# Shifted copies by 64-bit adds on GpSimd, with GpSimd's other work moved to VectorE, in a two-layer attention and MLP kernel

## The chip, the core and the metric

The kernel runs on one core of a Trainium2 chip. The metric is the device time of one execution in microseconds (us). The profile calls the engines PE (TensorE), ACT (ScalarE), DVE (VectorE), POOL (GpSimd) and SP (SyncE); PEld is TensorE's weight load.

## What is computed

The input `x` is 2048 rows of 512 bf16 numbers. Two layers follow, each an attention block and an MLP block with a residual sum around each; both layers use the same weights.

```python
x = x + _A_ref(_layernorm(x), A_wqkv, A_wo)
x = x + _B_ref(_layernorm(x), B_w1, B_b1, B_w2, B_b2)
x = x + _A_ref(_layernorm(x), A_wqkv, A_wo)
x = x + _B_ref(_layernorm(x), B_w1, B_b1, B_w2, B_b2)
...
scores = jnp.einsum("bhqd,bhkd->bhqk", q, k) * (Dh ** -0.5)
p = _softmax(scores, axis=-1)
o = jnp.einsum("bhqk,bhkd->bhqd", p, v)
...
h = _gelu(jnp.einsum("bsd,df->bsf", x, w1) + b1)
```

There are 32 heads of 16 columns, and the MLP is 1792 wide. Softmax is over 2048 keys for each of 2048 queries, 32 heads and 2 layers: 268 million exponentials.

## The kernel before

**Score blocks.** Queries are taken in segments of 512 (the last of the second layer in two of 256). A pass covers a segment and eight heads' worth of columns in pairs; its unit is a cell, a 128x512 block of scores: 128 keys against 512 columns of query. A matrix product of 32 rows (`score`, L1324) writes each cell to a PSUM bank; the kernel has 4096 of them. The queries it multiplies are masked copies of Q, so that one half of the head pair is zero (`qpad`, L1272).

**Two ways to an exponential.** Most cells are exponentiated by ACT (`exps`, L1725), two or three cells to an instruction. The cells of five key tiles per layer (`KD`) may take another path, called D here. DVE reads the cell from PSUM and makes a uint16 number by one multiply and add (`dfirst`, L1480): the bits of a bf16 number near the exponential. `dchain` then makes three more copies, the first plus 32, 64 and 96 in the bits: one operation adds `SHIFT` (32) to copy 0 for copy 1 (POOL, L1565), one adds 64 to copies 0 and 1 for copies 2 and 3 (DVE, L1570). A buffer (`DU`) holds the four copies of two cells, or of one. PE multiplies each of the four copies with V scaled by a weight of its own (`VC`, made by `vcopies`, L1255, on POOL; products at L1791) and sums them, so that the errors of the four approximations cancel in part. An ACT cell needs one such product, a D cell four. Where a round of four products has fewer than four, products with zeros fill it (L1799); L1312 are filling products that keep PE busy.

**The rest.** `ln` makes layer norms: statistics on DVE (L719, L721), variance plus epsilon (L724), its power -0.5 on POOL (L726), the shift (L729), and the normalized rows (`ln_tile`, L747) on POOL, or on DVE for the first four tiles and the last two (`quick`). The rows go through a DMA transpose that SP issues (L751). `norm` divides the attention output by its sums: transpose (L910), reciprocal (L913), product (L920, most of them on POOL), transpose back (L929). `proj`, `wo`, `hpair` and `ytile` are the dense products (L598), read out of PSUM by DVE; GELU is ACT's (L1076). `init` sets constants, among them the ones column of V (L623, L628), on POOL.

**What sets the order.** Nothing is decided on the chip: `_Sched` plays all work as threads at build time, each operation with a cost in us, a priority and the keys that it reads and writes, and picks for each engine what starts first. What comes out is a fixed program for each engine, with semaphore waits. The planner knows that a `port` operation of DVE and an operation of POOL hold each other up (`_ready`). `PICKS` names, for each 24 us of ACT's clock, one of the eleven rows of settings in `ORDERS`, so it chooses among orders. Which cells go to D is decided there too: `attach`, `solo` and `next_d` give a cell to D where a bank and a buffer are free and DVE is not too far behind. SP issues every DMA, 405 entries in its program with the branches.

Of the kernel before, what the change touches and what calls it, by code (L numbers as in the profile page):

```python
# [5 lines left out]
ALU = mybir.AluOpType  # L6
ACT = mybir.ActivationFunctionType
BF16 = mybir.dt.bfloat16
F32 = mybir.dt.float32
F16 = mybir.dt.float16  # L10
U16 = mybir.dt.uint16

# [6 lines left out]
NL = 2  # L19
# [15 lines left out]
LNP = 7  # L35
# [48 lines left out]
PSHIFT = 3  # L84
# [15 lines left out]
PICKS = (2, 0, 0, 6, 8, 2, 5, 1, 0, 5, 1, 0, 7, 5, 1, 0, 0, 7, 2, 5, 9, 1, 8, 7,  # L100
         4, 5, 7, 7, 7, 8, 5, 0, 5, 6, 9, 9, 7, 0, 5, 2, 5, 3, 3, 7, 4, 2, 7, 2,
         0, 9, 7, 7, 3, 3, 0, 2, 10, 10, 4, 4)
# [3 lines left out]
SHIFT = 32  # L106
VW = (0.83984375, 0.70703125, 0.59375)
# [106 lines left out]
class _Op:  # L214
    __slots__ = ("eng", "cost", "fns", "reads", "writes", "sem", "by", "tail", "prio", "mode", "slack", "late", "back", "port", "limit", "after")

    def __init__(self, eng, cost, fns, reads=(), writes=(), sem=None, by=1, tail=0.0, prio=None, mode="F", slack=None):
# [6 lines left out]
        self.port = eng == "dve" and self.writes[:1] != [] and self.writes[0].startswith(("OTT", "NMR"))  # L224
# [20 lines left out]
class _Sched:  # L245
# [152 lines left out]
    def run(self):  # L398
        while True:
# [67 lines left out]
            if e == "pool":  # L467
                self.pool_ops.append((start, start + cost))
# [7 lines left out]
def bass_interleave_layers__mha_block__dense_activation_gelu__prompt_kernel(  # L476
# [13 lines left out]
    NT = S // 128  # L490

    with ExitStack() as es:
# [48 lines left out]
        T["NHALF"] = sb([128, 4], F32, "nhalf")  # L541
        T["STATS"] = sb([128, NT, 6], F32, "stats")
# [45 lines left out]
class _Plan:  # L588
# [12 lines left out]
    def init(self):  # L601
# [14 lines left out]
        yield _Op("pool", 0.3, lambda e: e.memset(T["B2row"][:], 0.0), writes=["B2zero"])  # L616
        yield _Op("dve", 0.6, lambda e: e.memset(self.bank(PVB), 0.0), writes=["B.%d" % PVB])
# [3 lines left out]
        yield ("need", ("lnt", 3, 0))  # L621
        for a in range(0, self.NT, 4):
            yield _Op("pool", 0.65, lambda e, a=a: e.memset(T["V"][0][:, a:a + 4, :, 16:17], 1.0), writes=["V01"])  # L623
        yield ("need", ("otn", 0, (0, 0, 512), 3))
        for a in range(0, self.NT, 4):
            if a == 8:
                yield ("need", "v1back")
            yield _Op("pool", 0.65, lambda e, a=a: e.memset(T["V"][1][:, a:a + 4, :, 16:17], 1.0),  # L628
                      writes=[self.vone(1, a)] + (self.dukeys(DV1) if a >= 8 else ["PART.0.%d" % g for g in range(8)]))
        yield ("give", "v1ones")  # L630

# [80 lines left out]
    def ln(self, tiles, dst, dkeys, prio, quick=False, gate=None):  # L712
# [4 lines left out]
        for t in tiles:  # L717
# [8 lines left out]
        yield _Op("pool", 0.37 + 0.18 * n, lambda e: e.tensor_tensor(  # L726
            out=T["RSTD"][:, sl], in0=T["VARR"][:, sl], in1=T["NHALF"][:, 0:n], op=ALU.pow),
            reads=["VARR.%d" % c, "NHALF"], writes=["RSTD.%d" % c])
# [8 lines left out]
    def ln_tile(self, c, t, dst, dkeys, quick):  # L737
# [8 lines left out]
        eng, cost = ("dve", 0.4) if quick else ("pool", 0.77)  # L746
        yield _Op(eng, cost, lambda e: e.tensor_scalar(  # L747
# [130 lines left out]
    def norm(self, l, seg, g, b, part, final):  # L878
# [37 lines left out]
        pool = g < 6 and seg[2] == 512  # L916
        nb = w // 32
        for i, t in enumerate(ts):
            o3 = T["OTT"][:, o, 0:w].rearrange("p (k c) -> p k c", c=32)[:, :, 16 * t:16 * t + 16]
            yield _Op(*(("pool", 0.63 * w / 512) if pool else ("dve", 0.153 + 0.262 * w / 512)), lambda e, i=i, o3=o3: e.tensor_tensor(  # L920
# [297 lines left out]
    def setup_attention(self):  # L1218
# [25 lines left out]
        self.rush = self.base[(NL - 1, self.segs[-1][-3])]  # L1244
        self.duleft, self.open, self.starved, self.lend = {}, None, 0, 2

    def vcopies(self):
        T = self.T
        for l in range(NL):
            yield ("cond", lambda l=l: self.pv >= self.lead[l])  # L1250
            for j, kt in enumerate(KD[l]):
                yield ("need", ("V", l, kt, kt // 4))
                src = T["V"][l][:, kt, :, :].rearrange("p h c -> p (h c)")
                for i, w in enumerate(VW):
                    yield _Op("pool", 0.68, lambda e, j=j, i=i, w=w, src=src: e.tensor_scalar(  # L1255
# [5 lines left out]
    def qpad(self):  # L1261
        T = self.T
        for pi, (l, seg, g, kts, part, final) in enumerate(self.pas):
# [7 lines left out]
            for i, t in enumerate(ts):  # L1271
                yield _Op("pool", 0.27 + 0.42 * w / 512, lambda e, s=s, q=q, i=i, t=t, w=w: e.tensor_scalar(  # L1272
# [278 lines left out]
    def dchain(self, pair):  # L1551
# [3 lines left out]
        cells, du = pair["cells"], pair["du"]  # L1555
        yield ("cond", lambda: len(cells) == self.cap[du] or pair["full"] or self.starved)
# [6 lines left out]
        if self.s.clock["pool"] <= self.s.clock["dve"] + PSHIFT and len(pair["cells"]) == n:  # L1563
            a, b = U[:, 0, 0:n, :].rearrange("p j q -> p (j q)"), U[:, 1, 0:n, :].rearrange("p j q -> p (j q)")
            one = _Op("pool", 0.15 + 0.45 * n, lambda e, a=a, b=b: e.tensor_scalar(b, a, float(SHIFT), 1.0, op0=ALU.add, op1=ALU.mult),  # L1565
                      reads=key[0], writes=key[1])
        else:
# [333 lines left out]
```

## Time and profile before

| | |
|---|---|
| time, median of 3 runs | 1490.49 us (1490.07 to 1491.15) |
| span of the profiled execution | 1488.6 us |
| ACT busy | 1458.5 us (98%) |
| PE busy | 1439.3 us (97%) |
| DVE busy | 1369.4 us (92%) |
| POOL busy | 857.7 us (58%) |

The span runs from the first instruction to the last of one profiled execution; the 1.9 us between it and the median lie outside of it. A row of a group view gives line, engine, operation, what it writes and reads, the shapes and the count; then busy time in us and the mean of one in ns; then the idle time of its engine just before, and who ended it. A row of a line view gives the shortest, median and longest duration in ns. A row of a wait view reads: who waited, for whom, us in total, times, the longest.

### The profile page before, as it was taken

To read this page: it belongs to the slowest core of one execution; us is meant where nothing else is said; L and a number is where in the kernel's file an instruction comes from. 1 tells how busy PE (TensorE), PEld (TensorE's weight loads), DVE (VectorE), ACT (ScalarE), POOL (GpSimd) and SP (SyncE) were. 2 spreads that over 40 slices of the span, in tenths; PEclk is the share of its full clock that TensorE was granted. 3 is DMA by queue.
4 is the path that set the end of the run, shared out by engine and by line. 5 is a ranking of instruction groups with operands and counts; after the bars stand their busy time and mean duration, and the time that the engine had idled before them with its cause. 6 is when DMAs were issued, how large, how long until landed. Compare 5 with 4: busy or idle time off the path is not lost.

```text
span 1488.6 us, 46137 instructions
## 1 busy us (share of the span) xinstructions
PE 1439.3 (97%) x20011; PEld 433.5 (29%) x20011; DVE 1369.4 (92%) x2340; ACT 1458.5 (98%) x1438; POOL 857.7 (58%) x830
## 2 busy tenths in 40 slices
PE   8999999999999999999999999999999999999998
PEld 3222222222222222222222222222222222344445
DVE  6579999999999999999899999999999999998984
ACT  8999999999999999999999999999999999999995
POOL 5437656567465665556666567656556656654440
PEclk9999999999999999999999999999999999999999
DMA  5100001143120333114421144101143114411433
GB/s 161 40 2 2 2 2 44 37 136 109 29 52 30 117 109 81 39 30 127 118 63 30 46 124 121 34 2 37 40 148 99 37 30 130 143 40 35 148 110 95
DMA packets 145045, 103.38 MB, mean 69 GB/s; under 512 B 37069, under 2 KB 143822, under 8 KB 144846
## 3 DMA queue, kind: packets, MB, share of 16 engines
q1 hardware_dynamic: 144846, 100.44, 23.6%
q8 instruction: 160, 2.62, 0.7%
q14 instruction: 39, 0.32, 0.1%
HBM read 88.61 MB, written 4.19 MB: 62 GB/s over the span
## 4 chain that ended last, share of the span: by engine, by line
ACT 65%; PE 25%; DVE 8%; issue 1%; DMA 0%; SPq 0%; POOL 0%; ACTq 0%
ACT pt L1725 48%; PE ps L598 9%; PE ps L1324 8%; PE ps L1791 8%; ACT q L1725 5%; ACT v L1725 3%; DVE du L1480 3%; ACT g L1076 3%; ACT kt L1725 3%; DVE du L1570 2%; ACT g L1725 2%; ACT L1076 1%; ACT L1725 1%; DMA b1c<-in_B_b_dram 0%; DVE v L906 0%
## 5 line engine op out<-in xcount | busy, mean ns | idle before, releaser
L1725 ACT ACTIVATE pt<-ps 128x1024 bf16<-128x1024 f32 (+1 forms) x1106 | 1123.5, 1146 | 5.1 <-PE ps L1791 2.9
L1565 POOL TENSOR_SCALAR du<-du 128x1024 uint16<-128x1024 uint16 (+1 forms) x404 | 464.4, 1151 | 367.1 <-DVE du L1480 354.4
L1324 PE MATMUL ps<-qp,kt 32*128 32x512 bf16 x4096 | 553.7, 384 | 26.2 <-ACT pt L1725 13.5
L1480 DVE TENSOR_SCALAR du<-ps 128x512 uint16<-128x512 f32 x795 | 520.2, 680 | 31.6 <-PE ps L1324 28.9
L1791 PE MATMUL ps<-pt,v 128*17 128x512 bf16 (+1 forms) x2686 | 358.6, 359 | 5.5 <-ACT pt L1725 2.8
L1791 PE MATMUL ps<-du,vc 128*17 128x512 bf16 (+1 forms) x2646 | 345.0, 360 | 1.1 <-DVE du L1570 0.8
L1324 PEld LDWEIGHTS ps<-qp,kt 32*128 32x128 bf16 x4096 | 144.5, 91 | 596.1 <-ACT pt L1725 189.4
L1570 DVE TENSOR_SCALAR du<-du 128x2048 uint16<-128x2048 uint16 (+1 forms) x404 | 293.9, 739 | 5.0 <-POOL du L1565 4.8
L1799 PE MATMUL ps<-vc,zero 128*17 128x512 bf16 x909 | 179.0, 381 | 0.0
L1791 PE MATMUL ps<-du,v 128*17 128x512 bf16 (+1 forms) x882 | 160.8, 361 | 2.9 <-DVE xt L910 1.6
L1565 POOL TENSOR_SCALAR kt<-kt 128x1024 uint16<-128x1024 uint16 (+1 forms) x94 | 110.6, 1176 | 82.9 <-DVE kt L1480 77.0
L1480 DVE TENSOR_SCALAR kt<-ps 128x512 uint16<-128x512 f32 x186 | 123.3, 681 | 9.3 <-PE ps L1324 8.6
L598 PE MATMUL ps<-xf,wr 128*32 128x512 bf16 (+1 forms) x1888 | 130.6, 365 | 0.3 <-DVE g L1055 0.2
L1272 POOL TENSOR_SCALAR qp<-q,mask 128x512 bf16<-128x512 bf16 (+1 forms) x103 | 84.7, 822 | 63.2 <-PE ps L1324 60.8
L1791 PE MATMUL ps<-kt,vc 128*17 128x512 bf16 (+1 forms) x660 | 119.0, 348 | 1.4 <-DVE kt L1570 1.4
L598 PE MATMUL ps<-wr,g 128*32 128x512 bf16 x1600 | 117.3, 382 | 0.0
L1791 PEld LDWEIGHTS ps<-du,vc 128*17 128x17 bf16 x2646 | 90.9, 89 | 74.3 <-issue 45.5
L1791 PEld LDWEIGHTS ps<-pt,v 128*17 128x17 bf16 x2686 | 87.0, 88 | 87.7 <-issue 57.2
L1725 ACT ACTIVATE q<-ps 128x1024 bf16<-128x1024 f32 (+1 forms) x88 | 96.3, 1144 | 0.0
L1791 PE MATMUL ps<-kt,v 128*17 128x512 bf16 (+1 forms) x381 | 88.7, 363 | 0.9 <-DVE xt L910 0.6
L1565 POOL TENSOR_SCALAR v<-v 128x1024 uint16<-128x1024 uint16 x54 | 63.2, 1170 | 41.0 <-DVE v L1480 37.8
L1055 DVE TENSOR_SCALAR g<-ps,hb1t 128x512 bf16<-128x512 f32 (+1 forms) x112 | 78.8, 705 | 7.2 <-PE ps L598 7.0
(103 smaller groups left out, 1687.9 us busy)
## 6 DMA issues: line engine op xcount, KB each, us to landing
wr<-in_B_w_dram SPq DMA_DIRECT2D x256, 256.0 KB, 2.8
wr<-in_A_wqkv_dram SPq DMA_DIRECT2D x24, 256.0 KB, 2.8
wr<-in_A_wo_dram SPq DMA_DIRECT2D x18, 256.0 KB, 3.0
x<-in_A_x_dram SPq DMA_DIRECT2D x7, 512.0 KB, 4.3
kept<-x SPq DMA_DIRECT2D x4, 512.0 KB, 2.9
x<-kept SPq DMA_DIRECT2D x4, 512.0 KB, 4.0
out_dram<-x SPq DMA_DIRECT2D x16, 128.0 KB, 2.8
g<-in_A_wqkv_dram SPq DMA_DIRECT2D x3, 512.0 KB, 5.2
```

The source lines that it names most:

```text
L598: return [lambda e, a=a: e.matmul(out[32 * a:32 * a + 32, :], lhsT=lhsT[:, 32 * a:32 * a + 32], rhs=rhs, start=start, stop=stop, tile_posi ...
L1055: yield _Op("dve", 0.21 + n / 966, lambda e, fc=fc, pb=pb: e.tensor_scalar(T["G"][:, fc, q], pb, T["HB1T"][:, fc:fc + 1], None, op0=ALU.ad ...
L1076: lambda e, g=g: e.activation(out=g, in_=g, func=ACT.Gelu_apprx_tanh), reads=gk, writes=gk, prio=2)
L1272: yield _Op("pool", 0.27 + 0.42 * w / 512, lambda e, s=s, q=q, i=i, t=t, w=w: e.tensor_scalar(T["QP"][:, s, w * i:w * i + w], q, T["MASK"] ...
L1324: return (lambda e: e.matmul(o, lhsT=lhsT, rhs=rhs, start=True, stop=True, tile_position=(32 * a, 0)), ["K%d.%d.%d" % (l, gb, kt // 4), "Q ...
L1480: yield _Op("dve", 0.682, lambda e: e.tensor_scalar(u, self.bank(b), E_SCALE, E_BIAS, op0=ALU.mult, op1=ALU.add), reads=["B.%d" % b], writ ...
L1565: one = _Op("pool", 0.15 + 0.45 * n, lambda e, a=a, b=b: e.tensor_scalar(b, a, float(SHIFT), 1.0, op0=ALU.add, op1=ALU.mult), reads=key[0] ...
L1570: two = _Op("dve", 0.152 + 0.266 * n, lambda e: e.tensor_scalar(U[:, 2:4, 0:n, :], U[:, 0:2, 0:n, :], 2 * SHIFT, None, op0=ALU.add), reads ...
L1725: yield _Op("act", 0.065 + 0.4267 * n, lambda e, src=src, dst=dst: e.activation(out=dst, in_=src, func=ACT.Exp, scale=0.25), reads=["B.%d" ...
L1791: op.fns.append(lambda e, o=o, lhsT=q[0][0][m], rhs=q[0][1][:, n * m:n * m + n], a=a, st=st, sp=sp: e.matmul(o, lhsT=lhsT, rhs=rhs, start= ...
L1799: op.fns.append(lambda e, o=self.bank(b)[32 * a:32 * a + 17, :], rhs=rhs, a=a, st=not begun[a], sp=end: e.matmul(o, lhsT=T["ZERO"][:, 0:17 ...
```

## The change

Six things are changed.

1. `dchain` makes both shifts on POOL, as additions of a constant to 64-bit words: four 16-bit numbers at a time, `SHIFT` in each of the four. The first writes copy 1 from copy 0, the second copies 2 and 3 from copies 0 and 1. DVE's operation (L1570) is gone.
2. The masked query copies, the scaled V copies, all products of `norm`, all normalized rows and the ones columns are DVE's.
3. The power -0.5 is made on DVE from a first guess in integer bits and two steps of three operations. For the first four tiles and the last two it stays on POOL.
4. The add needs another library of POOL's than the power. An add on two words of a small tile (`LIB`), after the first four tiles, brings it in. After the last exponential and the last shift a memset stands in for the way back; the load stands in the program behind this memset and ahead of the last two powers.
5. The planner counts more DVE operations as `port`, and `PICKS` is another list.
6. The priority of layer norms goes from 7 to 0.3 (`LNP`), and that of the last segment's `norm` from 1 to 0.1.

```diff
-LNP = 7
+LNP = 0.3
...
-        self.port = eng == "dve" and self.writes[:1] != [] and self.writes[0].startswith(("OTT", "NMR"))
+        self.port = eng == "dve" and self.writes[:1] != [] and self.writes[0].startswith(("OTT", "NMR", "QP", "VC", "XLN", "PT", "V0", "V1")) and not self.reads[:1] == [] and not self.reads[0].startswith("B.")
...
         yield ("need", ("lnt", 3, 0))
+        yield _Op("pool", LOADS, lambda e: e.int64_add(T["LIB"][:, :], T["LIB"][:, :], 1), reads=["LIB"], writes=["LIB"])
         for a in range(0, self.NT, 4):
-            yield _Op("pool", 0.65, lambda e, a=a: e.memset(T["V"][0][:, a:a + 4, :, 16:17], 1.0), writes=["V01"])
+            yield _Op("dve", 0.25, lambda e, a=a: e.memset(T["V"][0][:, a:a + 4, :, 16:17], 1.0), writes=["V01"])
...
+        yield ("need", "exps")
+        yield ("cond", lambda: self.chains == 0)
+        yield _Op("pool", LOADS, lambda e: e.memset(T["LIB"][:].bitcast(F32), 0.0), reads=["LIB"], writes=["LIB"])
+        yield ("give", "stock")
...
+        if quick:
+            if self.phase[c // 4]:
+                yield ("need", "stock")
+            yield _Op("pool", 0.37 + 0.18 * n, lambda e: e.tensor_tensor(out=y, in0=v, in1=T["NHALF"][:, 0:n], op=ALU.pow),
+                      reads=vk + ["NHALF"], writes=yk)
+        else:
+            yield _Op("dve", 0.155, lambda e: e.tensor_scalar(y.bitcast(I32), v.bitcast(I32), -0.5, RGUESS, op0=ALU.mult, op1=ALU.add),
+                      reads=vk, writes=yk)
+        for k in () if quick else RSTEPS:
+            yield _Op("dve", 0.155, lambda e: e.tensor_tensor(out=a, in0=y, in1=y, op=ALU.mult), reads=yk, writes=ak)
+            yield _Op("dve", 0.155, lambda e, k=k: e.scalar_tensor_tensor(
+                out=b, in0=a, scalar=k[0], in1=v, op0=ALU.mult, op1=ALU.mult), reads=ak + vk, writes=bk)
+            yield _Op("dve", 0.155, lambda e, k=k: e.scalar_tensor_tensor(
+                out=y, in0=b, scalar=k[1], in1=y, op0=ALU.add, op1=ALU.mult), reads=bk + yk, writes=yk)
...
-        eng, cost = ("dve", 0.4) if quick else ("pool", 0.77)
-        yield _Op(eng, cost, lambda e: e.tensor_scalar(
+        yield _Op("dve", 0.41, lambda e: e.tensor_scalar(
...
-            yield _Op(*(("pool", 0.63 * w / 512) if pool else ("dve", 0.153 + 0.262 * w / 512)), lambda e, i=i, o3=o3: e.tensor_tensor(
+            yield _Op("dve", 0.153 + 0.262 * w / 512, lambda e, i=i, o3=o3: e.tensor_tensor(
...
-                    yield _Op("pool", 0.68, lambda e, j=j, i=i, w=w, src=src: e.tensor_scalar(
+                    yield _Op("dve", 0.42, lambda e, j=j, i=i, w=w, src=src: e.tensor_scalar(
...
-                yield _Op("pool", 0.27 + 0.42 * w / 512, lambda e, s=s, q=q, i=i, t=t, w=w: e.tensor_scalar(
+                yield _Op("dve", 0.15 + 0.262 * w / 512, lambda e, s=s, q=q, i=i, t=t, w=w: e.tensor_scalar(
...
-        if self.s.clock["pool"] <= self.s.clock["dve"] + PSHIFT and len(pair["cells"]) == n:
-            a, b = U[:, 0, 0:n, :].rearrange("p j q -> p (j q)"), U[:, 1, 0:n, :].rearrange("p j q -> p (j q)")
-            one = _Op("pool", 0.15 + 0.45 * n, lambda e, a=a, b=b: e.tensor_scalar(b, a, float(SHIFT), 1.0, op0=ALU.add, op1=ALU.mult),
-                      reads=key[0], writes=key[1])
-        else:
-            one = _Op("dve", 0.151 + 0.134 * n, lambda e: e.tensor_scalar(U[:, 1, 0:n, :], U[:, 0, 0:n, :], SHIFT, None, op0=ALU.add),
-                      reads=key[0], writes=key[1])
-        two = _Op("dve", 0.152 + 0.266 * n, lambda e: e.tensor_scalar(U[:, 2:4, 0:n, :], U[:, 0:2, 0:n, :], 2 * SHIFT, None, op0=ALU.add),
+        def words(i, k):
+            u = U[:, i:i + k, 0:n, :]
+            u = u.rearrange("p i j q -> p i (j q)") if k > 1 else u[:, 0, :, :].rearrange("p j q -> p (j q)")
+            return u.bitcast(I64)
+
+        yield _Op("pool", 0.151 + 0.2176 * n, lambda e: e.int64_add(words(1, 1), words(0, 1), SHIFT * ONES),
+                  reads=key[0], writes=key[1])
+        yield _Op("pool", 0.143 + 0.4352 * n, lambda e: e.int64_add(words(2, 2), words(0, 2), 2 * SHIFT * ONES),
                   reads=key[0] + key[1], writes=key[2] + key[3])
...
-            yield ("spawn", self.norm(l, seg, g, b, part, final), 1)
+            yield ("spawn", self.norm(l, seg, g, b, part, final), 0.1 if (l, seg) == (NL - 1, self.segs[-1][-1]) else 1)
```

`LOADS` is 6.5 and `ONES` is 0x0001000100010001. In the built programs the first copies of D cells (L1480) number 1089 before and 1173 after, in 552 chains before (537 of two cells, 15 of one) and 607 after (566 and 41); ACT's exponential instructions number 1379 and 1363.

32 lines of the change are left out of this document (20 added, 12 removed).

## The prediction

> **What bounds the kernel now.** I read the page's head first, then the waits of the bounding engine, then its busy time by stretch.
>
> ```profile
> span 1488.6 us, 46137 instructions
> PE 1439.3 (97%) x20011; PEld 433.5 (29%) x20011; DVE 1369.4 (92%) x2340; ACT 1458.5 (98%) x1438; POOL 857.7 (58%) x830
> ACT 65%; PE 25%; DVE 8%; issue 1%; DMA 0%; SPq 0%; POOL 0%; ACTq 0%
> ```
>
> Three engines are over 90%, so the shares alone decide nothing; the chain that ended last is ACT for 65%. The waits of ACT and the stretches say more:
>
> ```profile
> ACT xf L765 <- PE ps L758: 5.6, 1, 5.6
> ACT kt L765 <- PE ps L758: 5.2, 2, 4.8
> ACT pt L1725 <- PE ps L1791: 2.9, 7, 1.2
> ```
>
> ```profile
> 0.00:15.00 15.00, 11.54 (x211) 5.47 (x215) 10.03 (x32) 7.84 (x10) 7.78 (x21) 1.00 0.91 278
> 100.00:1400.00 1300.00, 1260.98 (x16972) 361.38 (x16971) 1248.64 (x2105) 1295.19 (x1269) 789.41 (x738) 1.00 0.23 66
> 1464.00:1488.60 24.60, 21.64 (x504) 13.87 (x504) 7.96 (x20) 8.07 (x16) 1.07 (x2) 1.00 0.28 80
> ```
>
> The columns are the stretch, then busy time of PE, weight loads, DVE, ACT and POOL, and the granted clock (1.00). Between 100 and 1400 us ACT is busy 1295.19 of 1300 us: it waits for nothing. Of its 30.1 us of idle time (1488.6 - 1458.5), 7.2 lie in the first 15 us and 16.5 after 1464, where layer norm and the last MLP run and no exponential is left. So **ACT's work sets the time**: a microsecond of exponentials taken from ACT is a microsecond of the kernel, as long as PE, DVE and POOL follow.
>
> **The change: what leaves ACT.** An exponential is made on ACT, or on the other path: DVE makes the first copy from PSUM (L1480), two operations make the three shifted copies, PE multiplies four times. In the built programs the first copies go from 1089 to 1173, so 84 score blocks of 128x512 leave ACT (3007 to 2923), and its exponential instructions go from 1379 to 1363. The rest of ACT (copies, GELU, 16 table loads) is the same count.
>
> ```profile
> L1725 ACT ACTIVATE pt<-ps 128x1024 bf16<-128x1024 f32 x921 | 888.3, 1075 | 3.3 <-PE ps L1791 2.4 <-PE ps L1324 0.3
> L1725 ACT ACTIVATE pt<-ps 128x1536 bf16<-128x1536 f32 x185 | 268.5, 1502 | 1.9 <-PE ps L1324 1.2 <-PE ps L1791 0.5
> ```
>
> ```profile
> 1451.22 6.42 ACT pt L1725 x7
> ```
>
> One block more costs 1.502 - 1.075 = 0.427 us. Seven two-block instructions follow each other in 6.42 us, 0.917 each, so an instruction costs 0.917 - 2 x 0.427 = 0.06 beside its blocks. ACT loses 84 x 0.427 + 16 x 0.06 = 35.9 + 1.0 = **36.9 us**.
>
> **What DVE loses and gains.**
>
> ```profile
> L1480 DVE TENSOR_SCALAR du<-ps 128x512 uint16<-128x512 f32 x795 | 520.2, 680 | 31.6 <-PE ps L1324 28.9
> L1570 DVE TENSOR_SCALAR du<-du 128x2048 uint16<-128x2048 uint16 (+1 forms) x404 | 293.9, 739 | 5.0 <-POOL du L1565 4.8
> L1570 DVE TENSOR_SCALAR kt<-kt 128x2048 uint16<-128x2048 uint16 (+1 forms) x94 | 69.6, 741 | 1.2 <-POOL kt L1565 1.2
> L1570 DVE TENSOR_SCALAR v<-v 128x2048 uint16<-128x2048 uint16 x54 | 39.6, 733 | 0.0
> ```
>
> ```profile
> L747 DVE TENSOR_SCALAR xln<-x,rstd,nmr x2: 408/410/411, 1470.1 to 1470.4; 128x512 bf16<-128x512 bf16 x2
> L729 DVE SCALAR_TENSOR_TENSOR nmr<-mv,rstd x25: 95/151/487, 5.7 to 1470.0; 128x4 f32<-128x4 f32 x10, 128x2 f32<-128x2 f32 x9, 128x1 f32<-128x1 f32 x6
> L920 DVE TENSOR_TENSOR ott<-xt,rc 128x256 bf16<-128x256 f32 x14 | 6.6, 469 | 0.2
> L617 DVE MEMSET ps<- x1: 485/485/485, 0.9 to 0.9; 128x512 f32 x1
> ```
>
> Gone: the second shift, 293.9 + 69.6 + 39.6 = 403.1 us. Added: 84 first copies at 0.680 (57.1); 103 masked query copies, 58 layer norm outputs and 30 scaled V copies, no such row on DVE but the 128x512 bf16 one at 0.410, which I take for all 191 (78.3); 42 output scalings at 0.469 (19.7); 19 reciprocal square roots of seven small operations at 0.151 (20.1); 8 memsets, a quarter of L617's elements, between nothing and 0.485, taken at 0.25 (2). Together 177, so DVE goes to 1369.4 - 403.1 + 177 = **1143 us, 79% of a 1452 us span**. It has slack where it had little. The layer norms' chain now waits in DVE's queue only, ahead of the other work by its new priority (0.3 for 7); SP issues the same 405 entries, its transposes waiting for DVE where they waited for POOL. I cost the later landing at nothing: the MLP that needs it runs beside the next segment's exponentials, and ACT's wait list shows no such wait today.
>
> **What POOL loses and gains.** Everything but the 64-bit adds leaves it: 566 pairs of blocks and 41 single ones, two adds each. There is no 64-bit row, so it is bounded by the nearest:
>
> ```profile
> L1565 POOL TENSOR_SCALAR du<-du x404: 616/1045/1534, 69.3 to 1455.7; 128x1024 uint16<-128x1024 uint16 x132, 128x512 uint16<-128x512 uint16 x3
> L920 POOL TENSOR_TENSOR ott<-xt,rc x42: 613/623/1056, 104.1 to 1243.3; 128x256 bf16<-128x256 f32 x42
> ```
>
> Undisturbed, 512 elements take 0.616 and 1024 take 1.045: 0.84 ns an element and 0.19 fixed. A pair's adds touch 256 and 512 words of 64 bits. If a 64-bit word costs one element: 0.40 + 0.62 = 1.02 us a pair. If it costs as its four 16-bit numbers: 1.045 + 1.90 = 2.95. I take it as two elements, its two 32-bit halves, 0.616 + 1.045 = **1.66 us**, because the f32 row shows that the engine's price goes by elements of up to 4 bytes (256 f32 pairs of operands, 512 elements read, in 0.623). POOL then has 566 x 1.66 + 41 x 1.0 = 981 us, 68%; the chain from first copy to last shift keeps its length (1.045 on POOL plus 0.68 on DVE before). It becomes the bound only above (1457 - 69) / (566 + 41 x 0.6) = **2.35 us a pair**, the shifts' stretch being 69 to 1457 us.
>
> [...]
>
> **The shared port.**
>
> ```profile
> 702.92 1.04 POOL L1565 TENSOR_SCALAR v<-v 128x1024 uint16<-128x1024 uint16 x1
> 703.48 0.49 DVE L729 SCALAR_TENSOR_TENSOR nmr<-mv,rstd 128x2 f32<-128x2 f32 x1
> ```
>
> A DVE operation with two SBUF inputs, 0.15 when free, started under a POOL operation and ended with it (703.97 against 703.96). The 366 moved or new DVE operations on SBUF (191 + 42 + 133) may all meet this. A random arrival finds POOL busy 68% of the time, with (0.616^2 + 1.045^2) / (2 x 1.66) = 0.44 us left: 0.30 us each, 110 us, DVE at 1253 us or 86%, still below the 92% of before. Bounds: nothing, or a whole second add each (1.05 us, 384 us, DVE 1527).
>
> **The ends.** A library is loaded for the adds after the first four reciprocal square roots (POOL idle then; the first shift is at 69 us) and loaded back before the last two.
>
> ```profile
> 1455.71 1.04 POOL L1565 TENSOR_SCALAR du<-du 128x1024 uint16<-128x1024 uint16 x1 [1.90 <-DVE du L1480]
> 1468.70 1.07 POOL L726 TENSOR_TENSOR rstd<-varr,nhalf 128x1 f32<-128x1 f32 x2 [11.95 <-DVE varr L724]
> ```
>
> Between the last shift and these square roots POOL sits idle 11.95 us; a load shorter than that costs nothing, a longer one lies whole on the final layer norm. No row shows a load; I take nothing, with up to 10 us kept for the range. [...]
>
> **The sum.** 1488.6 - 36.9 = 1451.7 us of span with ACT's 30 us of idle time unchanged. The runs' median, 1490.49, is 1.9 above the span: **1453.6 us**.
>
> **Rivals.**
>
> *PE is the limit.* Each block moved needs four multiplications for one.
>
> ```profile
> 704.47 1.05 PE L598 MATMUL ps<-wr,g 128*32 128x512 bf16 x16
> 705.45 0.39 PE L1324 MATMUL ps<-qp,kt 32*128 32x512 bf16 x4
> 705.77 0.39 PE L1791 MATMUL ps<-du,v 128*17 128x512 bf16 x4
> 706.00 0.39 PE L1791 MATMUL ps<-du,vc 128*17 128x512 bf16 x4
> ```
>
> A round of four takes 0.23, a score group 0.32 and 0.11 to switch back. In the built programs, PV products count 7363 before and 7615 after in full widths, but the zero products that fill their rounds go from 909 to 313: 86 rounds fewer (20 us), and 16 score groups fewer (7). PE loses 27 us, not 37: if it were the bound, 1463. Against it: ACT waits for PE 2.9 us in all. Chance 0.10.
>
> *The order doesn't fit the adds.* The order is fixed from the planner's costs, 0.586 + 1.013 = 1.60 a pair, where its costs of kept shifts (1.05, 0.684) match the rows' medians (1.045, 0.682). My 1.66 is 0.06 longer; if every one of 566 chains made PE, then ACT, wait for it, 34 us would go and 1488 remain; half of it, 1470. For it: the rounds are placed on the landing of their copies. Against: two score slots stand between PE and ACT. Chance 0.09, 1465 to 1488.
>
> *POOL becomes the bound (slower).* At the two-input row's price, (0.623 - 0.19) / 256 = 1.7 ns a 4-byte word, a pair takes 1.06 + 1.93 = 2.99, above the 2.35 from which it decides. POOL then needs 566 x 2.99 + 41 x 1.7 = 1762 us, with 69 before and 31 after: about 1860. [...] Against: the add has one tensor input and a constant. Chance 0.07.
>
> *The port fills DVE (slower).* If the mean wait is above (1420 - 1143) / 366 = 0.76 us (1420 being the span less some 32 us of ends), DVE is the bound; at a whole add each, 1527 us of DVE and some 1550 in time. Chance 0.05.
>
> **How the numbers follow.** The forecast as worked out has 0.69, its own range 1444 (the ends 10 us better used) to 1464 (a load that shows). With PE as the limit and the lower part of a misfit, 1444 to 1478 holds 8 in 10; the slower cases, far off at 1550 and 1860, are the rest. About 0.2% is what a measurement can tell from no change. Faster by more: 0.69 + 0.10 + most of 0.09 = 0.86; within: 0.02; slower: 0.07 + 0.05 = 0.12.
>
> **What would show it.** ACT busy about 1421 us and over 99% in each stretch from 100 us to the last exponential; POOL rows near 0.6 and 1.0 us, about 68% busy; DVE near 1253 us without any 128x2048 row; first copies 1173; the last square roots waiting for DVE, not for a load. The forecast is wrong if ACT shows idle time released by PE all along (then see what PE waits for: POOL says misfit or bound, DVE says port), if the adds take over 2.35 us a pair, or if DVE's small rows are some 0.8 us long.

## The result, and the profile after

The changed kernel takes **1479.47 us** (median of 4 runs, 1477.61 to 1481.0) against 1490.79 for the kernel before beside it: a ratio of 0.992, 95% interval 0.9906 to 0.9934. It is faster by 11 us. The forecast was 1453.6, with a range of 1444 to 1478, so the sign is right and a gain of 26 us is missing. The profiled execution has a span of 1476.7 us and a time of 1478.68.

The page's head, the busy times, and the chain that ended last, of the changed kernel:

```profile
span 1476.7 us, 45759 instructions
PE 1415.5 (96%) x19639; PEld 428.0 (29%) x19639; DVE 1219.1 (83%) x2246; ACT 1427.6 (97%) x1422; POOL 977.8 (66%) x1235
ACT 52%; PE 30%; DVE 14%; DMA 1%; POOL 1%; issue 1%; SPq 0%; ACTq 0%; DVEq 0%
```

ACT's busy time fell by 30.9 us, but the span only by 11.9: idle time of ACT rose from 30.1 to 49.1 us. PE and DVE have taken 11 points of the chain from ACT. The stretches (span, then PE, weight loads, DVE, ACT and POOL busy, clock) and the waits of ACT say where:

```profile
0.00:15.00 15.00, 11.56 (x202) 5.67 (x206) 9.78 (x35) 6.89 (x10) 4.53 (x18) 1.00 0.89 272
100.00:1400.00 1300.00, 1248.91 (x16818) 361.09 (x16818) 1101.25 (x1969) 1277.77 (x1264) 929.58 (x1162) 1.00 0.25 68
1452.00:1476.70 24.70, 21.84 (x504) 13.63 (x504) 8.38 (x22) 8.29 (x16) 1.13 (x2) 1.00 0.26 77
```

```profile
ACT pt L1751 <- PE ps L1351: 12.0, 24, 1.3
ACT kt L792 <- PE ps L785: 6.0, 1, 6.0
ACT xf L792 <- PE ps L785: 5.1, 1, 5.1
ACT pt L1751 <- PE ps L1817: 5.0, 3, 2.9
```

The two ends are as they were. Between 100 and 1400 us ACT now idles 22.2 us (1300 - 1277.77), where it idled 4.8 before. Over the whole span an exponential waited 24 times for its score products (L1351), 12.0 us in all. The kernel before has two such waits (its score products are L1324):

```profile
ACT pt L1725 <- PE ps L1324: 1.5, 2, 1.2
```

The new operations on POOL, by group, and then two of DVE's lines (shortest, median and longest duration):

```profile
L1596 POOL INT64_ADD du<-du x444 | 266.9, 602 | 318.5 <-DVE du L1507 290.9
L1598 POOL INT64_ADD du<-du x444 | 449.1, 1013 | 35.5
```

```profile
L753 DVE SCALAR_TENSOR_TENSOR rb<-ra,varr x38: 107/156/991, 20.0 to 1424.7; 128x4 f32<-128x4 f32 x20, 128x2 f32<-128x2 f32 x18
L1299 DVE TENSOR_SCALAR qp<-q,mask x103: 268/344/1222, 13.3 to 1386.2; 128x512 bf16<-128x512 bf16 x87, 128x256 bf16<-128x256 bf16 x16
```

The adds cost what was forecast (the line views give medians of 611 and 1037 ns). But an operation of DVE that takes 0.156 us in the median can take 0.991, and a masked copy of 0.344 can take 1.222. One place shows why, and what comes of it. From the timeline of the changed kernel, DVE, POOL, PE and ACT from 224 to 230 us (start, length, engine, operation; in brackets the idle time before it and what ended it):

```profile
224.20 0.61 POOL L1596 INT64_ADD du<-du  x1 [0.80 <-DVE du L1507]
224.79 2.08 POOL L1598 INT64_ADD du<-du  x2
224.75 1.22 DVE L1299 TENSOR_SCALAR qp<-q,mask 128x512 bf16<-128x512 bf16 x1
225.90 0.99 DVE L753 SCALAR_TENSOR_TENSOR rb<-ra,varr 128x4 f32<-128x4 f32 x1
227.53 1.28 DVE L1507 TENSOR_SCALAR kt<-ps 128x512 uint16<-128x512 f32 x2
228.96 0.40 PE L1351 MATMUL ps<-qp,kt 32*128 32x512 bf16 x4 [1.19 <-DVE kt L1507]
229.40 1.02 ACT L1751 ACTIVATE pt<-ps 128x1024 bf16<-128x1024 f32 x1 [1.26 <-PE ps L1351]
```

A masked copy starts 60 ns before one add ends, loses to the next, and waits that one out. The small operation behind it waits out the second (it ends at 226.89, the adds at 226.87). Of the 2.21 us of these two records, 1.7 are waiting (0.344 and 0.156 are their median lengths). So the two first copies read their PSUM banks some 1.7 us late; the score products need those banks and start after 1.19 us of idle PE; ACT has run dry for 1.26 us. **It is not DVE's capacity that is short**: DVE is 83% busy over the span. It is a delay in its queue, and ACT had less than half a microsecond of reserve against it here (1.7 us late, 1.26 idle).

The order was fixed at build time, so there is a second yardstick: the planner's own clock at the end of the order that it built. It is no time of the chip, but the same order run on the chip can be set against it, operation by operation. The kernel before plans 1483.5 us and runs 5 behind (span 1488.6). The changed kernel plans 1450.6 and runs **26 behind** (span 1476.7). The lag grows in steps, each right behind such a place: by 3 us between 200 and 250, by 4 to 5 between 500 and 650, by 3.5 between 850 and 900 and again between 1250 and 1300.

**The theory**, then: DVE's masked copies, normalized rows, products and small operations, all of them from SBUF to SBUF, wait out the adds that run (longest and median: masked copies 1.222 and 0.344 us, normalized rows 1.232 and 0.409, products 1.281 and 0.426, the small operation of L753 0.991 and 0.156); what is behind them in DVE's queue (the reading of PSUM) comes late, then PE, then ACT. Rivals: the adds don't fit the planned costs (prediction's second rival); DVE simply has more work in its queue; or the order itself is poor. `port`, the planner's word, stands below for these waits: the traces show the waits, and not what the two engines share. The rows above show the first half; what a wait costs in what stands behind it is for the experiments.

### The profile page after: what moved, and what is told of

The parts are those of the page before. It is cut to its first block, busy times and chain, and to the rows that moved or that the text cites. A ratio compares the mean times of both kernels' runs of the same rounds, so it can differ in the third digit from the quotient of the medians.

```text
span 1476.7 us, 45759 instructions
## 1 busy us (share of the span) xinstructions
PE 1415.5 (96%) x19639; PEld 428.0 (29%) x19639; DVE 1219.1 (83%) x2246; ACT 1427.6 (97%) x1422; POOL 977.8 (66%) x1235
## 4 chain that ended last, share of the span: by engine, by line
ACT 52%; PE 30%; DVE 14%; DMA 1%; POOL 1%; issue 1%; SPq 0%; ACTq 0%; DVEq 0%
ACT pt L1751 41%; PE ps L607 10%; PE ps L1351 10%; PE ps L1817 9%; DVE du L1507 6%; ACT g L1102 3%; ACT kt L1751 2%; ACT q L1751 2%; ACT v L1751 2%; DVE kt L1507 1%; DVE v L1507 1%; DVE xln L774 1%; DVE stats L734 1%; DMA wr<-in_B_w_dram 1%; ACT L1102 1%
## 5 line engine op out<-in xcount | busy, mean ns | idle before, releaser
L1751 ACT ACTIVATE pt<-ps 128x1024 bf16<-128x1024 f32 (+1 forms) x1096 | 1103.9, 1136 | 18.2 <-PE ps L1351 12.0
L1507 DVE TENSOR_SCALAR du<-ps 128x512 uint16<-128x512 f32 x858 | 572.4, 683 | 115.9 <-PE ps L1351 112.3
L1351 PE MATMUL ps<-qp,kt 32*128 32x512 bf16 x4096 | 553.8, 384 | 37.4 <-ACT pt L1751 11.4
L1596 POOL INT64_ADD du<-du x444 | 266.9, 602 | 318.5 <-DVE du L1507 290.9
L1598 POOL INT64_ADD du<-du x444 | 449.1, 1013 | 35.5
L1817 PE MATMUL ps<-du,vc 128*17 128x512 bf16 (+1 forms) x2856 | 324.2, 360 | 1.4 <-ACT pt L1751 0.5
L1351 PEld LDWEIGHTS ps<-qp,kt 32*128 32x128 bf16 x4096 | 144.7, 91 | 601.3 <-issue 175.0
L1817 PE MATMUL ps<-pt,v 128*17 128x512 bf16 (+1 forms) x2630 | 283.9, 360 | 5.3 <-ACT pt L1751 2.1
L1817 PE MATMUL ps<-du,v 128*17 128x512 bf16 (+1 forms) x952 | 142.4, 360 | 3.9 <-DVE xt L937 1.2
L1598 POOL INT64_ADD kt<-kt x104 | 105.1, 1011 | 8.3
L1596 POOL INT64_ADD kt<-kt x104 | 62.4, 600 | 60.8 <-DVE kt L1507 57.4
L1817 PE MATMUL ps<-v,vc 128*17 128x512 bf16 (+1 forms) x402 | 90.3, 350 | 0.0
L1507 DVE TENSOR_SCALAR v<-ps 128x512 uint16<-128x512 f32 x115 | 77.5, 682 | 11.9 <-PE ps L1351 11.6
L1751 ACT ACTIVATE kt<-ps 128x1024 bf16<-128x1024 f32 (+1 forms) x71 | 78.5, 1134 | 2.5 <-PE ps L1351 0.6
```

The costliest lines, as they stand in the source:

```text
L1351: return (lambda e: e.matmul(o, lhsT=lhsT, rhs=rhs, start=True, stop=True, tile_position=(32 * a, 0)), ["K%d.%d.%d" % (l, gb, kt // 4), "Q ...
L1507: yield _Op("dve", 0.682, lambda e: e.tensor_scalar(u, self.bank(b), E_SCALE, E_BIAS, op0=ALU.mult, op1=ALU.add), reads=["B.%d" % b], writ ...
L1596: yield _Op("pool", 0.151 + 0.2176 * n, lambda e: e.int64_add(words(1, 1), words(0, 1), SHIFT * ONES), reads=key[0], writes=key[1])
L1598: yield _Op("pool", 0.143 + 0.4352 * n, lambda e: e.int64_add(words(2, 2), words(0, 2), 2 * SHIFT * ONES), reads=key[0] + key[1], writes=k ...
L1751: yield _Op("act", 0.065 + 0.4267 * n, lambda e, src=src, dst=dst: e.activation(out=dst, in_=src, func=ACT.Exp, scale=0.25), reads=["B.%d" ...
L1817: op.fns.append(lambda e, o=o, lhsT=q[0][0][m], rhs=q[0][1][:, n * m:n * m + n], a=a, st=st, sp=sp: e.matmul(o, lhsT=lhsT, rhs=rhs, start= ...
```

## First experiments: is it the port?

The fences of edits below show only the parts of the lines that differ.

**The adds cut to nothing.** In `a_short` the order, the semaphores and every operation stay; each add touches two words. PE multiplies copy 0 in place of the others, so that nothing reads what isn't written.

```diff
-e.int64_add(words(1, 1), words(0, 1), SHIFT * ONES)
+e.int64_add(words(1, 1)[:, 0:2], words(0, 1)[:, 0:2], SHIFT * ONES)
-e.int64_add(words(2, 2), words(0, 2), 2 * SHIFT * ONES)
+e.int64_add(words(2, 1)[:, 0:2], words(0, 1)[:, 0:2], 2 * SHIFT * ONES)
-(ws, U[:, i, jj, :].bitcast(BF16),
+(ws, U[:, 0, jj, :].bitcast(BF16),
```

> The changed kernel in the same order, with every 64-bit add cut to two words; PE multiplies copy 0 four times, so the three shifted copies are left out. GpSimd then holds the shared port for almost no time and no copy is late. If VectorE's waits behind GpSimd's adds delay the reads of PSUM and through them PE and ACT (port theory), the time falls by nearly all that the forecast missed: to 1452 to 1458 us, and VectorE's rows of two SBUF inputs are at their free length (0.15 us for the small ones). If the copies land later than the order holds (misfit theory), it falls to the same. If PE is the limit, or the order itself leaves ACT gaps, it stays at 1474 to 1480.

Measured: **1457.77 us** (ratio 0.9778, 0.9763 to 0.9792). The page of `a_short`:

```profile
span 1455.2 us, 45759 instructions
PE 1408.8 (97%) x19639; PEld 429.2 (29%) x19639; DVE 1172.2 (81%) x2246; ACT 1421.5 (98%) x1422; POOL 236.5 (16%) x1235
```

The order is fine: it runs 4.6 us behind its plan, like the kernel before. All but 4 of the missing 26 us hang on the adds' length. ACT's 1421.5 us is the forecast's 1421.6; the other 6 us in the changed kernel are put down (an estimate) to records of exponentials that start after a wait and no longer overlap the one before: in its trace a two-block exponential behind idle time adds 1.023 us to ACT's busy time in the median (84 of them), one that overlaps the record before it (by 0.144) adds 0.917. DVE's busy time falls by 46.9 us with the same 2246 operations: it was waiting.

The edit alone does not tell a wait at the port from a copy that lands late, since it takes away both. The waits of PE tell them apart. First two rows of the changed kernel, then two of `a_short`:

```profile
PE ps L1351 <- DVE du L1507: 8.6, 22, 0.8
PE ps L1817 <- POOL du L1598: 1.3, 3, 0.7
```

```profile
PE ps L1351 <- DVE du L1507: 1.4, 4, 0.5
ACT pt L1751 <- PE ps L1351: 1.7, 4, 0.9
```

In the changed kernel PE's score products wait 8.6 us for banks that DVE has yet to read, and its other products 1.3 us for copies of POOL's. Without the adds' length the first wait falls to 1.4, and ACT's wait for score products from 12.0 to 1.7.

**The adds made to fit the plan.** In `a_planned` the second add is 18 words shorter for each copy, which takes 0.06 us from a pair, the misfit that the prediction saw (copies 2 and 3 are read as copy 1).

```diff
-e.int64_add(words(2, 2), words(0, 2), 2 * SHIFT * ONES)
+e.int64_add(words(2, 2)[:, :, 0:128 * n - 18], words(0, 2)[:, :, 0:128 * n - 18], 2 * SHIFT * ONES)
-(ws, U[:, i, jj, :].bitcast(BF16),
+(ws, U[:, min(i, 1), jj, :].bitcast(BF16),
```

> The changed kernel in the same order, with the second add short of 18 words in each of its two copies, so that a pair of adds takes about 0.06 us less, what the order holds for it; PE multiplies copy 1 in the place of copies 2 and 3, which stay incomplete. Misfit theory (a pair longer than the order holds by 0.06 us, 607 times): most of the missing 25 us come back, 1455 to 1463. Port theory: waits shorten by a few hundredths only, 1474 to 1481. PE as the limit: no change, 1477 to 1481.

Measured: 1476.63 us (0.9906, 0.9891 to 0.9921), 2.8 us under the changed kernel, of 26. As the main cause the misfit is out.

**The square roots made without the port.** Seven small operations of DVE make a reciprocal square root (19 times, 133 operations). The planner's list of operations that share the port has the masked copies, the V copies, the normalized rows, the shifts and the products of `norm`, but not these (keys VARR, RSTD, RA, RB). In `b_newton` all 133 are memsets (the 38 of L753 take 0.060 to 0.062 us). (The scale of the normalized rows is then the 20 that the last memset writes, not 1 as the expectation has it.)

```diff
-lambda e: e.tensor_tensor(out=a, in0=y, in1=y, op=ALU.mult)
+lambda e: e.memset(a, 1.0)
...
-e.scalar_tensor_tensor(out=y, in0=b, scalar=k[1], in1=y, op0=ALU.add, op1=ALU.mult)
+e.memset(y, 20.0)
```

> The changed kernel in the same order, with the 133 small operations of the reciprocal square root on VectorE replaced by memsets of the same tiles (the norms' scale is left out and is 1). A memset reads nothing from SBUF, and the changed kernel's memsets of the ones columns show no wait beside GpSimd's adds. Port theory, the unplanned waits being those of these small operations (the planner's list of port operations does not name their tiles): 10 to 18 us less than the changed kernel, 1462 to 1470. If the planned waits (masked queries, normalized rows, output scalings) are the cause: 1473 to 1478. Misfit or PE as the limit: 1477 to 1481.

Measured: **1463.19 us** (0.9816, 0.9801 to 0.983). Sixteen of the 26 us are gone with operations that make up 133 of DVE's 2246.

**The adds in halves.** If an operation waits out one running add, shorter adds should help: `d_halves` makes the second add as two.

```diff
-lambda e: e.int64_add(words(2, 2), words(0, 2), 2 * SHIFT * ONES)
+[lambda e, i=i: e.int64_add(words(i, 1), words(i - 2, 1), 2 * SHIFT * ONES) for i in (2, 3)]
```

> The changed kernel in the same order, with the second add as two instructions of half the words, so that no hold of the port is longer than about 0.61 us in the place of 1.04; GpSimd does about 0.17 us more per chain, 607 times, some 100 us in all. Port theory: the longest waits are cut to 0.6, and a third to a half of the missing 25 us comes back, 1466 to 1474, unless the copies, which land 0.17 us later, take it. Misfit theory: each chain is 0.17 us later still, 1485 to 1520. PE as the limit: no change.

Measured: 1482.27 us (0.9946, 0.9929 to 0.9963), slower than the change. A miss, and it pointed at something. From the timeline of `d_halves`, DVE and POOL:

```profile
128.63 5.16 DVE L946 TENSOR_TENSOR ott<-xt,rc 128x256 bf16<-128x256 f32 x1
133.71 0.34 DVE L1299 TENSOR_SCALAR qp<-q,mask 128x512 bf16<-128x512 bf16 x1
```

```profile
128.20 0.61 POOL L1598 INT64_ADD du<-du  x1
128.79 1.20 POOL L1598 INT64_ADD kt<-kt  x2
129.96 1.20 POOL L1596 INT64_ADD du<-du  x2
131.13 2.37 POOL L1598 INT64_ADD du<-du  x4
```

An output scaling of 0.43 us stood **5.16 us**, behind the add that ran and eight more that followed with no gap, until POOL had nothing left to do. A masked copy at 1183 us stood 3.35 in the same way. The lag behind the plan jumps by 4 us in each of these two stretches; without those 8 us the run would lie at 1474, at the edge of what was expected.

## Second experiments: work, or waits? And can the plan know?

**Work kept, port avoided.** `b_newton` took away work of DVE too. In `e_aggr` the first of each seven is a memset and six are `bn_aggr` operations, as long as the originals but without a wait for POOL (in the changed kernel the longest of 64 took 0.182 us, the median 0.172).

```diff
-lambda e: e.tensor_tensor(out=a, in0=y, in1=y, op=ALU.mult)
+lambda e: e.bn_aggr(T["RA"][:, 2 * c:2 * c + 2], T["STATS"][:, c, :])
```

> The order of the change, and all its adds; of the 133 operations of the reciprocal root on VectorE only the work is kept, not the kind: the first of each seven becomes a memset, the other six become aggregations of 0.17 us into scratch, which did not wait for GpSimd in any trace so far (the scale of the rows becomes 20: that part of the computation is left out). If the roots cost time because they wait out an add on the shared port: 1461 to 1467, within 4 us of the kernel with memsets in their place (1463.2), and the span is 10 to 14 us behind the plan made at build. If they cost time because they are work in VectorE's queue (133 x 0.17 = 23 us of it): 1474 to 1481, as the change (1479.5).

Measured: **1464.76 us** (0.9823, 0.9808 to 0.9837). The line view of `e_aggr` beside the row of L753 above:

```profile
L753 DVE BATCH_NORM_AGGREGATE rb<-stats x38: 144/173/385, 19.7 to 1410.2; 128x2 f32<-128x6 f32 x38
```

The median operation is longer than the one that it replaces (0.173 for 0.156), the longest 0.385 and not 0.991, and 14.7 us are gone. It is the wait, not the work. It is also not the layer norm's result that came late: PE waits 0.7 us for normalized rows in the changed kernel and 0.5 in `e_aggr`, while ACT's wait for score products goes from 12.0 to 3.9 us.

**The planner told.** `c_listed` adds four names to the planner's list and keeps the picks; `c_tuned` searches the picks anew.

```diff
-"XLN", "PT", "V0", "V1"))
+"XLN", "PT", "V0", "V1", "VARR", "RSTD", "RA", "RB"))
```

> One line is changed: the planner is told that the rows of the root (VARR, RSTD, RA, RB) share the port, so that it starts them only where no add runs; the order comes out otherwise, and with the old picks the plan made at build gets longer, from 1450.6 to 1479.8 us. If the time lost on the chip was unplanned port waits: the chip stays within 4 to 9 us of the plan (the change: 26 behind), span 1484 to 1489, time 1485 to 1491: slower than the change by some 8 us, though no operation is added. If it was lost elsewhere: the gap stays at 20 to 28, time 1500 to 1510.

> The same line, and the 60 picks of the order searched anew for it: the plan made at build ends at 1457.2 us. All of the change's work is in it. If the time lost was unplanned port waits: span 4 to 9 us behind the plan, 1461 to 1466, time 1463 to 1468, some 13 us below the change and 25 below the kernel before. If it was lost elsewhere, the gap stays at 20 to 28: time 1479 to 1487, no better than the change.

Measured: `c_listed` **1488.72 us** (0.9981, 0.9972 to 0.999; 10 runs), some 7 behind its plan by the median, as expected. `c_tuned` **1478.73** (0.9924, 0.9907 to 0.9941) for 1463 to 1468: a clear miss, 19.6 behind. Its trace puts 7 of these into one place, seen here in the timeline of `c_tuned` (DVE, ACT, then POOL) and its stretch from 140 to 150 us:

```profile
136.54 5.74 DVE L944 TENSOR_TENSOR ott<-xt,rc 128x256 bf16<-128x256 f32 x1
143.59 1.45 ACT L1749 ACTIVATE pt<-ps 128x1536 bf16<-128x1536 f32 x1 [4.87 <-PE ps L1349]
```

```profile
136.15 0.61 POOL L1594 INT64_ADD kt<-kt  x1
136.74 1.04 POOL L1596 INT64_ADD du<-du  x1
137.76 1.04 POOL L1596 INT64_ADD kt<-kt  x1
138.77 1.20 POOL L1594 INT64_ADD du<-du  x2
139.95 2.05 POOL L1596 INT64_ADD du<-du  x2
```

```profile
140.00:150.00 10.00, 6.81 (x56) 1.36 (x57) 7.31 (x11) 4.63 (x4) 5.31 (x6) 0.50 0.00 0
```

The plan had left a gap for this scaling: it starts at 136.51 in the plan, and the next add at 136.70. But **nothing on the chip holds that gap**. The planner moves an add's time, which settles the order within each engine, and emits no wait for it. POOL, whose inputs were there, went straight on through six adds; DVE stood for 5.74 us, PE for 4.95 (138.0 to 142.9) and ACT for 4.87. The granted clock was 0.99 between 130 and 140 us and 0.50 between 140 and 150.

## Third experiments: hold the gap

`c_locked` is `c_tuned` with a wait on POOL: ahead of an add that the plan puts behind the start of a port operation of DVE, POOL waits for the DVE operation before that one. `before` is DVE's count when the port operation is emitted.

```diff
+            before = self.P.cnt["dve"]
+            if e == "pool":
+                for a, b, n in self.port_ops[-4:]:
+                    if a < start:
+                        self.P.wait("pool", "dve", n)
             ev = self.P.group(e, op.fns, op.reads, op.writes, op.sem, op.by)
...
-                self.port_ops.append((start, start + cost))
+                self.port_ops.append((start, start + cost, before))
```

`g_tuned` gives the planner the measured prices of the adds (0.178 and 0.169 for the fixed 0.151 and 0.143) and searches the picks again; `g_locked` is the same order with POOL's waits. `l_own` puts the waits into the changed kernel and alters nothing else; `l_all` extends them there to the square roots' operations.

> The order of c_tuned, with one thing added: GpSimd waits, ahead of an add that the plan puts behind the start of a VectorE operation on the port, until VectorE has finished the operation before that one, so that a row of adds can't run ahead of the plan. If 7 of c_tuned's 18.5 us behind its plan came from the one output scaling that stood 5.74 us behind six adds at 136.54 us (and from the clock of 0.50 after it): no operation of VectorE on the port over 1.4 us, 9 to 13 us behind the plan of 1457.2, time 1468 to 1473. If that row was no cause: 1477 to 1482. If GpSimd's waits cost more than they save: above 1482.

> The planner knows of the root's rows and has the adds' measured prices (0.027 us more for each add); the 60 picks searched anew, plan 1455.6 us. No waits are added. If the 11 us that remain behind the plan in c_listed and e_aggr come from adds that end some 26 ns later than planned, so that VectorE meets the handover between two adds: 4 to 8 us behind, time 1461 to 1466. If they come from other waits (the plan's gap for VectorE is only an intention, GpSimd runs ahead of it): 10 to 13 behind, 1467 to 1471; with one row of adds as in c_tuned 5 to 7 more.

> g_tuned's order with GpSimd's waits of c_locked. If the port's waits are what is left and the plan's gaps need to be held: 3 to 7 us behind the plan of 1455.6, time 1460 to 1465, the fastest of the versions that do all the work. If the waits hold the adds up and the copies come later: 10 to 20 behind, 1467 to 1478.

> The changed kernel's own order and picks, not an operation or a place altered; only GpSimd's waits of c_locked are added, for the operations that the planner knows to share the port (the root's rows not among them). If most of the loss is the root's rows, which the plan starts under running adds, waits can't help them: 1474 to 1480, 20 to 27 us behind the plan of 1450.6. If it is GpSimd running ahead of the plan, whatever the operation: 1460 to 1468.

> The same order, and GpSimd waits for the root's rows too (VARR, RSTD, RA, RB), 133 + 25 operations more. An add that the plan puts behind a root's row can then no longer start ahead of it, but one that the plan lets run when the row arrives still has to be waited out: part of the root's 15 us comes back if GpSimd's running ahead matters there, 1465 to 1473; if the plan's overlaps are all of it, 1473 to 1480 as l_own; above 1482 if the waits put the adds behind the whole of each root.

| kernel | plan ends, us | span, us | behind, us | port waits (operations, us) | time, us | ratio, 95% interval |
|---|---|---|---|---|---|---|
| before | 1483.5 | 1488.6 | 5.1 | 14, 4 | 1490.79 | 1 |
| change | 1450.6 | 1476.7 | 26.1 | 115, 51 | 1479.47 | 0.9906 to 0.9934 |
| a_short | 1450.6 | 1455.2 | 4.6 | 2, 0 | 1457.77 | 0.9763 to 0.9792 |
| e_aggr | 1450.6 | 1462.2 | 11.6 | 83, 34 | 1464.76 | 0.9808 to 0.9837 |
| c_tuned | 1457.2 | 1476.8 | 19.6 | 95, 44 | 1478.73 | 0.9907 to 0.9941 |
| c_locked | 1457.2 | 1464.2 | 7.0 | 92, 31 | 1465.62 | 0.9812 to 0.9842 |
| g_tuned | 1455.6 | 1469.1 | 13.5 | 118, 51 | 1471.32 | 0.9844 to 0.9879 |
| g_locked | 1455.6 | 1463.1 | 7.5 | 95, 34 | **1464.09** | 0.9796 to 0.9832 |
| l_own | 1450.6 | 1473.1 | 22.5 | 110, 41 | 1473.18 | 0.9865 to 0.9894 |
| l_all | 1450.6 | 1473.8 | 23.2 | 114, 42 | 1474.44 | 0.9866 to 0.9899 |

Plan and span are of one profiled execution, the time is the median of all. A port wait is counted where a DVE operation of the planner's list or of the square roots is over 0.08 us above the lower quartile of its own group; how the groups are cut moves a count by up to three.

- `c_locked` takes 13 us from `c_tuned` without another change, more than the 7 of the one place: 1465.62, under the 1468 to 1473 expected. The timeline of `c_locked` has the same scaling at 0.51 us. Now the add that begins at 136.93 takes 1.20 us where 1.04 is usual: it is the add that waited.

```profile
136.72 0.51 DVE L949 TENSOR_TENSOR ott<-xt,rc 128x256 bf16<-128x256 f32 x1
137.16 1.88 DVE L1510 TENSOR_SCALAR du<-ps 128x512 uint16<-128x512 f32 x3
```

```profile
136.93 1.20 POOL L1601 INT64_ADD du<-du  x1
138.11 1.04 POOL L1601 INT64_ADD kt<-kt  x1
```

- `g_tuned`, 1471.32, is 13.5 behind, next to the 10 to 13 expected if prices are not the cause: truer costs don't hold a gap either. `g_locked`, the same order with the waits, is 7.5 behind, half a microsecond over what was expected. It is the fastest kernel here that does all the work: 1464.09, ratio 0.9814, **27 us below the kernel before and 15 below the change**. (Whether the kernel before would gain from another search of its picks was not tried.) Its page:

```profile
span 1463.1 us, 45994 instructions
PE 1412.2 (97%) x19687; PEld 428.1 (29%) x19687; DVE 1196.4 (82%) x2237; ACT 1427.1 (98%) x1421; POOL 969.6 (66%) x1217
```

- `l_own` takes 6.3 us from the change, just more than expected; `l_all` no more than `l_own`. So in the change's own order the waits did not help the square roots: the plan itself starts them under running adds, because it doesn't know that they wait. In that plan, 82 of the 158 operations on the four keys start more than 0.15 us ahead of the end of an add, and 5 of the 295 operations that it knows to share the port; in the plan of `c_tuned` none of the 158 does. They need the list and a new order, and the order then needs the waits.

## Why the prediction was wrong

**The step that failed** is "The shared port". It priced the waits as DVE's busy time (110 us, DVE at 86%) and found them hidden by DVE's slack, and "The sum" then left ACT's idle time unchanged. The waits were shorter in all than forecast, 51 us, and DVE's 83% is under the 86%. But an operation in order delays what stands behind it: a PSUM bank read late is a score product late, and an exponential late (at 224 us: 1.7 us late, 1.19 of idle PE, 1.26 of idle ACT). With `a_short` and `e_aggr` the 25.9 us between 1453.6 and 1479.47 divide into 14.7 for waits of the square roots, 7.0 for what else hangs on the adds' length, and 4.2 that remain when the adds are cut to two words. The 7.0 are, by the traces, mostly waits of the other moved operations; copies that land late were not taken out apart, and PE waits some 2 us for them in the changed kernel. Nor is a microsecond of waiting worth the same everywhere: `e_aggr` has 32 waits and 17 us of waiting less than the change, and these cost 14.7 us; the 83 waits and 34 us that are left, most of them of operations that the plan sets around its adds, cost at most 7.0. The fourth rival had the right resource and the wrong price: it asked from which mean wait DVE would be full (0.76 us), where 115 waits with a mean of 0.44 were enough. That the time came out only 1.5 us above the range is luck: the range reached up to 1478 for PE as the limit and for a misfit of prices, and neither was the cause.

**What leaves ACT**: right, to 0.1 us (1421.5 in `a_short`). There ACT is busy 1291.83 of the 1300 us between 100 and 1400, so the rule that its work sets the time holds as soon as the waits are gone.

**DVE's work**: 1143 us forecast, 1172.2 without port waits in `a_short`. 29 us too low, which did no harm. The forecast took off and put on whole durations, but records of DVE overlap the ones before them (in the changed kernel 1499 of 2246, by 0.082 us in the median). Summed, the durations fall from 1529.8 to 1289.8 us, by 240 where 226 were forecast; the busy time, which counts an overlap once, falls by 197.

**POOL's adds**: right. A pair takes 0.611 + 1.037 = 1.65 us for 1.66, and POOL 977.8 us in all, 972 of them adds, for 981. A 64-bit word with a constant costs what two elements did in the trace before: (1.037 - 0.611) / 256 = 1.66 ns for 2 x 0.84. The rival that POOL is the bound (2.99 us a pair) is out. With one tensor input and a constant on POOL, `g_locked` (1464.09 us) is 27 us faster than the kernel before; a kernel with the change's other parts and the shifts on VectorE was not run. What the adds cost here is not POOL's time but DVE's order.

**The ends**: right. The built program has a library load ahead of the first add and one ahead of the last two square roots on POOL. Neither has a row of its own; the trace of the changed kernel shows two `MODIFY_POOL_CONFIG` of 0.019 us at 7.1 us and two of 0.011 at 1442.9. The waits of POOL there:

```profile
POOL rstd L746 <- DVE varr L739: 14.1, 1, 14.1
POOL lib L632 <- issue: 7.3, 1, 7.3
```

The last square roots wait 14.1 us for DVE. The 7.3 us, in which POOL waited for nothing that the profile shows, end with the first add at 14.6; the first shift comes at 70.1, so they cost nothing. That the first load fills them is an estimate, from its place in the program. How long the load back takes is not seen: the square roots start at 1457.03, 0.09 us after DVE's operation ends, so none of it shows beyond the 14.1.

**PE as the limit**: no. PE's busy time fell by 23.8 us (27 forecast; the 0.11 to switch is 0.105 in the trace before, 0.321 from a round to a score group for 0.216 from round to round, medians), and `a_short`, with the same 19639 products of PE, ends 21.7 us earlier; there ACT is 98% busy with PE at 97%.

**The order doesn't fit the adds**: not for the 0.06 us (`a_planned` gains 2.8 us by it, and `g_tuned`, planned with the measured prices, is still 13.5 behind), but its place was well chosen: the order does not fit, because the plan's gaps are not kept and the square roots are not in it.

What stays open: of the 7.5 us that `g_locked` is behind its plan, 5 are also there in the kernel before; whether the rest can be had was not tried, nor were halves of the adds with POOL's waits.

## What to carry to other kernels

A wait in the middle of an engine's queue is not a share of its busy time: ask what stands behind it, and how much reserve the bounding engine has there (at 224 us here, under half a microsecond). Where an order is planned at build time, set the chip's trace against the plan: an order that runs 5 us behind and one that runs 26 behind have different faults. And a gap that a plan leaves on one engine for the sake of another need not be there on the chip: in `c_tuned` nothing held it, and the scaling at 136.5 us took 5.74 us; in `c_locked` a semaphore wait of POOL held it, and the scaling took 0.51.

## What the runs showed of the hardware

- In the changed kernel, 110 of the moved DVE operations and those of the square roots started with over 0.27 us of an add left. Of these, 106 ended 0.01 to 0.28 us after the add, 4 (all of the square roots) 0.41 to 0.92 us before its end. The wait was the rest of the add less some 0.14 us in the median.
- Not every handover is won. In twelve traces of kernels with full adds, a DVE operation of these kinds started within 66 ns of an add's end, with the next add right behind, 69 times, and 36 times it waited that next add out too (the masked copy at 224.75). What decides between the two was not found. Of those that started earlier, 7 did, all with 73 to 266 ns of the add left. Three of these 7, of some 2400 operations that met an add in these traces, lost to a whole row of adds, for 3.0, 4.7 and 5.3 us; each had started 186 to 266 ns before an add's end. In `c_locked`, `g_locked` and `l_all`, with POOL's waits, neither was seen, in `l_own` one lost handover.
- Two adds that follow each other overlap by some 25 ns in the records (in `c_tuned` 1.04 us each, 2.05 for two).
- In `c_tuned` PE stood still from 138.0 to 142.9 us. The granted clock was 1.00 between 120 and 130, 0.99 between 130 and 140 and 0.50 between 140 and 150, where single products of L1815 take 0.60 us for 0.38 before the stop; in `c_locked`, without the stop, it was 1.00 from 130 to 150. In `c_tuned` the lag behind the plan grew from 5.3 us at 143 to 7.4 at 150.
- Operations of DVE that read PSUM, `bn_stats`, `bn_aggr`, transposes and reciprocals did not wait for adds in the changed kernel: the longest `bn_aggr` of 64 took 0.182 us (median 0.172), the longest `bn_stats` of 64 0.695 (0.682), the longest reciprocal of 64 0.256 (0.239), the longest transpose out of PSUM (L937, 44) 0.717 (0.705) and back (L955, 28 of 128x512) 0.714 (0.711), the longest sum with a PSUM bank (L1132, 32) 0.690 (0.678). Of the first copies, 702 started with over 0.15 us of an add left; the longest of these took 0.694 us (median 0.683).
